# Ten weight conversions moved into the first pair's tiles, the first pair's input sums on VectorE and GpSimd, and routing's vector steps moved to the next pair

## The chip, the cores and the metric

The kernel runs on one core of a Trainium2 chip. The core has TensorE (PE; its weight loads are shown apart as PEld), VectorE (DVE), ScalarE (ACT), GpSimd (POOL) and SyncE (SP, which here issues most DMAs). The metric is device time in microseconds, the median of several runs. All times below are microseconds from the start of the profiled execution, unless it is said otherwise.

## What is computed

Three stages follow each other, in float32:

```python
# 1. linear attention: 4 batches x 8 heads, 576 positions, head size 64, 128 features
proj = q @ w_phi;  proj -= max(abs(proj));  phi = concat(exp(proj), exp(-proj))   # the same for k
kv = phi_k.T @ v;  z = sum(phi_k);  attn = (phi_q @ kv) / (phi_q @ z + 1e-6)
x = attn, 2304 tokens x 512
# 2. dense gated layer, 512 -> 1536 -> 512
g = x @ w_gate;  x2 = (g * sigmoid(g) * (x @ w_val)) @ w_out
# 3. mixture of 8 experts, 512 -> 1024 -> 512: each token goes to its best expert
e = argmax(x2 @ gate);  y = prob[e] * sigmoid(x2 @ output_gate)[e] * (relu(x2 @ w1[e]) @ w2[e])
```

## The kernel before

**Float32 on TensorE by halves.** A float32 operand is split into a rounded high half and a low half, `low = x - high`, and a product is three matmuls: high x high, high x low, low x high. Such a split is called a cut: one ScalarE copy for the high half (`cut`, line 544), one subtraction on VectorE or GpSimd for the low half (`cut_lo`, line 541).

**The attention part** (`first_part`, line 669). Sixteen units, each of two heads of a batch: `qk_mm` (12 small matmuls to a group, three groups, line 330), `qk_sub` (maximum and subtraction on VectorE from PSUM, lines 336 and 339), `k_exp`, `kv_mm`, `tq_mm`, `tq_exp`, `num_mm`, `normalise`, `tx_mm`, and then the attention's output x is stored by pieces. x has six blocks of 384 tokens. Pieces of blocks 0 and 1 stay in SBUF as halves (`x_hi`, line 427, ScalarE; `x_lo`, line 431, VectorE); the others go to DRAM (`x_keep`, `x_store`).

**The weights' conversion** stands between these steps. The weights of the dense layer arrive as 36 chunks of 512 KB (64-bit words, 12 f-tiles of 128 hidden columns times gate, value and output weights). For each: `conv_load` (SyncE, into one of three buffers `ST`), `conv_scale` (ScalarE, to a PSUM bank, line 443), `conv_round` (ScalarE line 452 or GpSimd line 450, into one of four buffers `CP`), `conv_sign` (GpSimd line 458 or VectorE line 460), `conv_bits` (VectorE, line 464) and `conv_add` (GpSimd, line 468). The results lie in `WR[f]`.

The order of all this is written out: `Plan.op` registers each step with its dependencies, and `PLAN_TABLE` lists the steps in the order in which they are issued; a number of 1000 or more takes the step's other engine (`alt`). Each engine runs its steps in that order. Buffers are shared: the input sums S1 and S2 lie where `ST[0]`, `ST[1]` and `CP[0]` were (step `third`, after the last conversions), the weight sums `SS` where the units' inputs were.

**The dense layer** runs over pairs of blocks: (0, 1), (2, 3) and (4, 5), by a scheme with seven products of half size in place of eight (`product`, names A11, A12, S1 to S4, A22; six matmuls of 384 columns each, lines 584 to 586). It needs sums of the weights (`weight_sum`, line 553, four per f-tile) and sums of the input blocks (`SUMS`: S1, S2, S3 and A22). For pair 0 the input sums are matmuls with plus and minus identity matrices into PSUM (`sum_mm`, line 514), then a ScalarE copy (line 760) and a VectorE subtraction (`sum_lo`, line 519). For pairs 1 and 2 they are float32 subtractions on VectorE (`x_sums2`, lines 523 and 533).

`pair(p, rest)` runs the 12 f-tiles of a pair; tile 0 of pair 0 is already in `first_part`, written out product by product, with a cut of its weights for each slot (`pcut`, `sums_of`, `cut_22`). Per tile there are 42 matmuls of 384 columns for the products and nine of 512 columns for the layer's output (`o_tiles`, lines 475 to 477) of block 2p; the hidden values of block 2p+1 are stored to DRAM (`hd`, line 660) and used in `down(p)`, which forms that block's output: 12 steps of nine matmuls, with the input sums of the next pair and the cuts of the hidden values (`cut`, line 541) between them.

**Routing** of a block's tokens is a list of small steps: `post_log` three times, `post_mm`, `post_sum` (transposes and logits), `route_a` (twenty small instructions, most on VectorE), `route_b` (six small matmuls and six VectorE instructions). `down(p)` takes one of them off the list `todo` for each of its steps from the third on (`fill(1)`). Between the products of `pair` the function `rest` calls `fine(2)`, which issues two single instructions of the list `todo`; it is called three times in a tile (group g = 0, 1, 2), in the tiles after the first. `fine(1000)` at the start of `down` issues what is left.

The instructions of `pair` and `down` are not in a written order: the scheduler of the tile framework places them on each engine. The instructions of an engine wait in order.

Of the kernel before, what the change touches and what calls it, by code (L numbers as in the profile page):

```python
# [8 lines left out]
F32 = mybir.dt.float32  # L9
# [44 lines left out]
class Arena:  # L54
# [138 lines left out]
def kernel(ctx, tc, qT, kT, v1, wphi, w1cat, wlog, mw1, mw2, consts, out):  # L193
# [231 lines left out]
    def x_hi(u, piece, b):  # L425
        c, j, o, w = piece
        ACT.activation(XH[:, j, u % 4, o:o + w], PS[:, b, c:c + w], AF.Copy)

    def x_lo(u, piece, b):
        c, j, o, w = piece  # L430
        DVE.tensor_tensor(out=XL[:, j, u % 4, o:o + w], in0=PS[:, b, c:c + w],
                          in1=XH[:, j, u % 4, o:o + w].bitcast(F32), op=ALU.subtract)
# [983 lines left out]
    def down(p):  # L1416
# [8 lines left out]
        for i, f in enumerate(order_):  # L1425
# [18 lines left out]
            if i >= 2:  # L1444
                fill(1)
# [77 lines left out]
```

## Time and profile before

| | us |
|---|---|
| median of 3 runs | 867.95 (867.4 to 870.95) |
| profiled execution | 871.13 |
| its span (first to last instruction) | 869.4 |

Busy time over the span: TensorE 841.3 us (97%), weight loads 735.7 (85%), VectorE 583.6 (67%), ScalarE 501.8 (58%), GpSimd 446.8 (51%). The attention part ends at about 182 us, the first pair's tiles at about 291, its down stage at about 324; pair 1 ends with its down stage at about 474, pair 2 at about 655, and the experts take the rest.

How to read it: these shares are means over stages with different limits, so the busy time has to be asked for by stretch. A busy TensorE is one with a matmul in it, since matmuls overlap. A group of instructions by line gives its count, its busy time, the mean duration of one in nanoseconds, and the idle time of the engine just before, with what ended it. The granted clock of TensorE is 1.00 at its higher level and 0.50 at its lower.

### The profile page before, as it was taken

To read this page: it belongs to the slowest core of one execution; us is meant where nothing else is said; L and a number is where in the kernel's file an instruction comes from. 1 tells how busy PE (TensorE), PEld (TensorE's weight loads), DVE (VectorE), ACT (ScalarE), POOL (GpSimd) and SP (SyncE) were. 2 spreads that over 40 slices of the span, in tenths; PEclk is the share of its full clock that TensorE was granted. 3 is DMA by queue.
4 is the path that set the end of the run, shared out by engine and by line. 5 is a ranking of instruction groups with operands and counts; after the bars stand their busy time and mean duration, and the time that the engine had idled before them with its cause. 6 is when DMAs were issued, how large, how long until landed. Compare 5 with 4: busy or idle time off the path is not lost.

```text
span 869.4 us, 17427 instructions
## 1 busy us (share of the span) xinstructions
PE 841.3 (97%) x6745; PEld 735.7 (85%) x6746; DVE 583.6 (67%) x1105; ACT 501.8 (58%) x936; POOL 446.8 (51%) x421
## 2 busy tenths in 40 slices
PE   8899999989999989999999999999999999999995
PEld 6888998979999869999986999898778888888884
DVE  6898998856556596666659777676686434344693
ACT  4768887846555655555666555555433434344883
POOL 3788888876666655666655666536302212120110
PEclk9999999989999999999999999999999999999998
DMA  8776876710000231000031000006701332010650
GB/s 242 183 236 193 234 241 204 230 50 28 19 19 28 91 109 47 19 19 20 30 95 59 2 1 1 1 0 255 303 1 50 131 99 110 24 51 1 245 208 11
DMA packets 30876, 84.58 MB, mean 97 GB/s; under 512 B 6462, under 2 KB 15678, under 8 KB 29504
## 3 DMA queue, kind: packets, MB, share of 16 engines
q1 hardware_dynamic: 27216, 73.57, 26.5%
q0 software_dynamic: 3200, 9.48, 3.2%
q8 instruction: 55, 0.90, 0.4%
q10 hardware_dynamic: 368, 0.33, 0.2%
q14 instruction: 37, 0.30, 0.1%
HBM read 79.13 MB, written 17.86 MB: 112 GB/s over the span
## 4 chain that ended last, share of the span: by engine, by line
PE 73%; DVE 13%; issue 6%; DMA 3%; ACT 3%; POOL 1%; SPq 0%; POOLq 0%; DVEq 0%; ACTq 0%
PE banks L584 10%; PE banks L586 9%; PE banks L585 9%; PE banks L477 5%; PE banks L476 5%; PE banks L475 5%; PE banks L1204 3%; PE banks L1205 3%; PE banks L1206 3%; PE banks L1220 3%; PE banks L1218 3%; PE banks L1219 3%; DVE arena L336 3%; PE banks L330 2%; PE banks L391 2%
## 5 line engine op out<-in xcount | busy, mean ns | idle before, releaser
L544 ACT ACTIVATE r_dense<-arena 128x512 fp32r<-128x512 f32 (+1 forms) x168 | 100.7, 610 | 135.1 <-PE banks L585 106.4
L553 POOL TENSOR_TENSOR arena<-arena 128x256 f32<-128x256 f32 x144 | 106.6, 751 | 105.5 <-DVE r_dense L541 96.9
L541 POOL TENSOR_TENSOR r_dense<-arena,r_dense 128x512 fp32r<-128x512 f32 x72 | 97.1, 1349 | 60.0 <-ACT r_dense L544 58.4
L541 DVE TENSOR_TENSOR r_dense<-arena,r_dense 128x512 fp32r<-128x512 f32 (+1 forms) x102 | 76.2, 747 | 58.4 <-ACT r_dense L544 58.3
L1194 ACT ACTIVATE arena_r<-arena 128x512 fp32r<-128x512 f32 x64 | 40.3, 633 | 104.5 <-PE banks L1205 49.5
L1197 DVE TENSOR_TENSOR arena_r<-arena,arena_r 128x512 fp32r<-128x512 f32 x64 | 44.2, 693 | 81.4 <-ACT arena_r L1194 79.6
L586 PE MATMUL banks<-arena_r,r_dense 128*128 128x384 f32 x288 | 97.8, 340 | 0.3 <-POOL r_dense L541 0.3
L585 PE MATMUL banks<-arena_r,r_dense 128*128 128x384 f32 x288 | 97.5, 338 | 0.0
L584 PE MATMUL banks<-arena_r,r_dense 128*128 128x384 f32 x288 | 96.8, 343 | 0.6 <-ACT arena L609 0.4
L606 DVE TENSOR_TENSOR banks<-arena,banks 128x384 f32<-128x384 f32 x140 | 77.7, 555 | 9.4 <-ACT arena L609 5.0
L1155 POOL DMA_INDIRECT out_dram<-arena x20 | 21.2, 1059 | 109.6 <-ACT arena L1251 39.6
L613 DVE SCALAR_TENSOR_TENSOR arena<-arena,banks 128x384 f32<-128x384 f32 x70 | 38.8, 554 | 55.3 <-ACT arena L612 54.9
L1150 POOL DMA_INDIRECT ov_gather<-x2d,arena x20 | 21.4, 1071 | 98.3 <-PE banks L1164 57.9
L584 PEld LDWEIGHTS banks<-arena_r,r_dense 128*128 128x128 f32 x288 | 54.4, 189 | 4.8 <-DVE r_dense L606 1.5
L585 PEld LDWEIGHTS banks<-arena_r,r_dense 128*128 128x128 f32 x288 | 54.5, 189 | 3.4 <-issue 0.6
L586 PEld LDWEIGHTS banks<-arena_r,r_dense 128*128 128x128 f32 x288 | 54.6, 190 | 1.8 <-POOL r_dense L541 1.0
L609 ACT ACTIVATE arena<-banks 128x384 f32<-128x384 f32 x105 | 50.5, 482 | 7.2 <-PE banks L586 7.2
L336 DVE TENSOR_REDUCE arena<-banks 128x6 f32<-128x768 f32 x48 | 45.8, 954 | 12.9 <-PE banks L330 11.0
L584 PE MATMUL banks<-ov_pair,r_dense 128*128 128x384 f32 x144 | 51.3, 356 | 0.5
L1204 PE MATMUL banks<-arena_r 128*128 128x512 f32 x128 | 50.2, 393 | 0.8 <-ACT arena_r L1194 0.8
L1206 PE MATMUL banks<-arena_r 128*128 128x512 f32 x128 | 50.0, 391 | 0.0
L1205 PE MATMUL banks<-arena_r 128*128 128x512 f32 x128 | 50.0, 390 | 0.0
(220 smaller groups left out, 2367.7 us busy)
## 6 DMA issues: line engine op xcount, KB each, us to landing
arena<-mw SPq DMA_DIRECT2D x16, 2048.0 KB, 8.4
ov_conv<-w1cat SPq DMA_DIRECT2D x24, 512.0 KB, 5.9
arena<-w1cat SPq DMA_DIRECT2D x12, 512.0 KB, 6.5
arena<-v SPq DMA_DIRECT2D x16, 325.0 KB, 6.6
hd<-arena SPq DMA_DIRECT2D x24, 192.0 KB, 1.8
x2d<-arena SPq DMA_DIRECT2D x18, 256.0 KB, 2.8
arena<-qT SPq DMA_DIRECT2D x15, 288.0 KB, 4.9
arena<-kT SPq DMA_DIRECT2D x15, 288.0 KB, 5.3
```

What stands on the lines that cost most here:

```text
L336: DVE.tensor_reduce(out=MX, in_=ps, axis=AX.X, op=ALU.max, apply_absolute_value=True)
L541: eng.tensor_tensor(out=w[1], in0=src, in1=w[0].bitcast(F32), op=ALU.subtract)
L544: ACT.activation(w[0], src, AF.Copy)
L553: POOL.tensor_tensor(out=o, in0=x, in1=y, op=op)
L584: PE.matmul(ps, w[0][:, c], xh[:, k, :], start=(start and k == 0), stop=False, skip_group_check=True)
L585: PE.matmul(ps, w[0][:, c], xl[:, k, :], start=False, stop=False, skip_group_check=True)
L586: state["pe"] = PE.matmul(ps, w[1][:, c], xh[:, k, :], start=False, stop=(k == 1), skip_group_check=True).ins
L606: DVE.tensor_tensor(out=out_, in0=x, in1=y, op=op)
L609: ACT.activation(out_, x, AF.Copy)
L1204: PE.matmul(ps, wh[:, c], XQH[:, k, :], start=(k == 0), stop=False)
L1205: PE.matmul(ps, wh[:, c], XQL[:, k, :], start=False, stop=False)
L1206: PE.matmul(ps, wl[:, c], XQH[:, k, :], start=False, stop=(k == 3))
```

## The change

Three things.

1. **Ten of the 36 chunks are converted in pair 0's tiles 1 to 10**, one in each (`LATE`, all of f-tiles 8 and 9, two of f-tile 10, two others). Their steps are those of the other chunks, on fixed engines: scaling and rounding on ScalarE after product S3, sign and bits on VectorE after S1, the addition on GpSimd and the next chunk's load at the tile's end. They use bank 7, buffer `ST[2]` and `CP[1..3]`. The first of these loads is issued behind `first_part`.
2. **The input of pair 0 stays in float32** (`X01`, in the place of the weights of f-tiles 8 and 9, with one sum's place `XT1` in f-tile 10's). A piece is one copy (ScalarE, or VectorE). The sums are four float32 subtractions and seven cuts (`less`, `finish`), on VectorE or GpSimd as the table says; the `sum_mm` matmuls and the identity matrices are gone. Weight sums, cuts and the last low halves get the other engine as an alternative.
3. **`down(0)` and `down(1)` issue routing steps only in their steps 2 to 6**: that takes the logits, and leaves `route_a` and `route_b` to the tiles of the next pair. In the last pair `fine` issues three instructions at a call in place of two.

With this goes a new `PLAN_TABLE`. By its entries the steps of `first_part` are, before and after: `conv_scale` 36 and 26 (ScalarE); `conv_round` 16 and 6 (ScalarE), 20 and 20 (GpSimd); `conv_sign` 26 and 21 (GpSimd), 10 and 5 (VectorE); `conv_bits` 36 and 26 (VectorE); `conv_add` 36 and 26 (GpSimd); input halves 12 ScalarE and 12 VectorE before, copies 9 ScalarE and 3 VectorE after; sums of the input 4 of `sum_mm` on TensorE with 4 copies (ScalarE) and 4 low halves (VectorE) before, 4 subtractions (GpSimd), 7 high halves (ScalarE) and 7 low halves (2 VectorE, 5 GpSimd) after; weight sums 8 GpSimd before, 3 GpSimd and 5 VectorE after; low halves of weights 4 VectorE and 5 GpSimd before, 3 and 6 after.

```diff
+    LATE = [24, 25, 27, 28, 26, 30, 31, 29, 33, 35]
+    EARLY = [i for i in range(3 * NFT) if i not in LATE]
+    def stage(i):
+        return ST[2 if i in LATE else EARLY.index(i) % 3]
+    def rounded(i):
+        return CP[1 + LATE.index(i) % 3 if i in LATE else EARLY.index(i) % 4].bitcast(I32)
...
+    def conv_late(f, g):
+        if not 0 < f <= len(LATE):
+            return
+        i = LATE[f - 1]
+        if g == 0:
+            conv_scale(i, 7)
+            conv_round(i, ACT)
+        elif g == 1:
+            conv_sign(i, 7, DVE)
+            conv_bits(i, 7)
+        else:
+            conv_add(i)
+            if f < len(LATE):
+                conv_load(LATE[f])
...
-    SUMS = dict(S1=("+01", "-00"), S2=("+11", "-01", "+00"), A22=("+10", "-11", "+01", "-00"), S3=("+11", "-01"))
-    def sum_mm(name, b): ...
-    def sum_lo(name, b): ...
+    o = offs["WR"] + 8 * 1536
+    X01 = [A[:, o + j * 1536:o + (j + 1) * 1536].rearrange("p (k t) -> p k t", k=4) for j in range(2)]
+    XT1 = A[:, o + 3072:o + 3840].rearrange("p (k t) -> p k t", k=2)
...
+        def finish(name, src, reads):
+            op("ACT", 85, lambda: ACT.activation(opx[name][0], src, AF.Copy), reads, [("fin", name)], due=140)
+            def low(eng):
+                eng.tensor_tensor(out=opx[name][1], in0=src, in1=opx[name][0].bitcast(F32), op=ALU.subtract)
+            op("DVE", 105, lambda: low(DVE), reads + [("fin", name)], [("fin2", name)], due=140, alt=("POOL", 195, lambda: low(POOL)))
+        def less(dst, x, y, reads, writes):
+            def f(eng):
+                eng.tensor_tensor(out=dst, in0=x, in1=y, op=ALU.subtract)
+            op("DVE", 105, lambda: f(DVE), reads, writes, due=130, alt=("POOL", 195, lambda: f(POOL)))
...
     first_part()
+    conv_load(LATE[0])
...
     def rest(p, f, g):
+        if p == 0:
+            conv_late(f, g)
...
-        fine(2)
+        fine(3 if p == NP - 1 else 2)
...
-            if i >= 2:
+            if i >= 2 and (end or i < 7):
                 fill(1)
```

## Rows read from the trace of the kernel before

**Rows 1.** Busy time by stretch (us, PE, PEld, DVE, ACT, POOL; clock; DMA share)

```profile
100.00:120.00 20.00, 20.00 (x482) 18.86 (x480) 19.08 (x33) 17.27 (x35) 18.47 (x12) 1.00 0.88 253
182.00:190.00 8.00, 7.68 (x25) 6.94 (x26) 3.21 (x6) 2.88 (x6) 5.98 (x8) 0.58 0.07 25
220.00:240.00 20.00, 20.00 (x109) 18.98 (x108) 11.42 (x22) 11.69 (x24) 12.37 (x14) 1.00 0.05 20
```

**Rows 2.** The chain that ended last, near 155 (start, us, what)

```profile
154.56 5.18 DMA arena<-w1cat
```

**Rows 3.** TensorE's matmuls near 182 (start, us, what, idle before)

```profile
182.31 0.69 PE L586 MATMUL banks<-arena_r,arena_r 128*128 128x384 f32 x1 [2.33 <-POOL arena_r L541]
182.80 0.52 PE L584 MATMUL banks<-arena_r,ov_pair 128*128 128x384 f32 x1
183.12 0.52 PE L585 MATMUL banks<-arena_r,ov_pair 128*128 128x384 f32 x1
```

**Rows 4.** Busy time by stretch in the two down stages

```profile
303.50:326.00 22.50, 19.62 (x97) 14.30 (x96) 22.29 (x46) 13.04 (x24) 11.60 (x10) 1.00 0.34 105
446.00:476.00 30.00, 28.29 (x140) 21.34 (x139) 25.68 (x50) 18.47 (x35) 16.20 (x13) 1.00 0.21 60
```

**Rows 5.** VectorE's groups by line, 0 to 183.7 (count, busy us, mean ns)

```profile
L464 DVE SCALAR_TENSOR_TENSOR arena<-banks,arena 128x512 int32<-128x512 int32 x36 | 24.3, 681 | 0.1
L431 DVE TENSOR_TENSOR arena_r<-banks,arena_r 128x192 fp32r<-128x192 f32 (+1 forms) x12 | 4.6, 414 | 0.0
L519 DVE TENSOR_TENSOR arena_r<-banks,arena_r 128x768 fp32r<-128x768 f32 x2 | 1.9, 952 | 0.0
```

**Rows 6.** VectorE's groups by line, 296 to 326

```profile
L523 DVE TENSOR_TENSOR arena_r<-arena,arena_r 128x768 fp32r<-128x768 f32 x3 | 4.3, 1434 | 0.0
```

**Rows 7.** GpSimd's groups by line, 0 to 183.7

```profile
L468 POOL TENSOR_TENSOR arena<-arena 128x512 int32<-128x512 int32 x27 | 34.9, 1298 | 11.3 <-DVE arena L464 9.1 <-DVE banks L398 1.9
L458 POOL TENSOR_SCALAR arena<-ov_conv 128x512 int32<-128x512 f32 x17 | 33.7, 1984 | 2.2 <-DMA ov_conv<-w1cat 2.1
L553 POOL TENSOR_TENSOR arena<-arena 128x256 f32<-128x256 f32 x14 | 11.1, 798 | 0.4
```

**Rows 8.** Two VectorE lines, shortest, median and longest ns

```profile
L541 DVE TENSOR_TENSOR r_dense<-arena,r_dense x4: 772/1153/1862, 164.2 to 179.2; 128x512 fp32r<-128x512 f32 x4
L339 DVE TENSOR_TENSOR r_att<-banks,arena x24: 957/957/959, 7.6 to 142.9; 128x768 f32<-128x768 f32 x24
```

**Rows 9.** ScalarE's groups by line, 0 to 183.7

```profile
L443 ACT ACTIVATE banks<-ov_conv 128x512 f32<-128x512 f32 x24 | 15.7, 659 | 2.1 <-DVE arena L339 0.9 <-DVE r_att L339 0.6 <-DMA ov_conv<-w1cat 0.4
L427 ACT ACTIVATE arena_r<-banks 128x192 fp32r<-128x192 f32 (+1 forms) x12 | 4.3, 388 | 1.5 <-PE banks L405 1.4
L760 ACT ACTIVATE arena_r<-banks 128x768 fp32r<-128x768 f32 x2 | 1.6, 801 | 0.7 <-PE banks L514 0.7
```

**Rows 10.** TensorE around sixteen matmuls of the sums

```profile
156.48 3.03 PE L514 MATMUL banks<-arena_r,arena_r 128*128 128x384 f32 x16
159.35 0.49 PE L376 MATMUL banks<-arena 128*128 128x128 f32 x3
```

**Rows 11.** ScalarE, the same cut in two tiles of pair 0

```profile
219.78 0.63 ACT L544 ACTIVATE r_dense<-arena 128x512 fp32r<-128x512 f32 x1 [1.41 <-PE banks L585]
229.17 0.63 ACT L544 ACTIVATE r_dense<-arena 128x512 fp32r<-128x512 f32 x1 [1.40 <-PE banks L585]
```

**Rows 12.** SyncE's stores of hidden blocks in pair 0

```profile
224.77 9.71 SPq L660 DMA_DIRECT2D hd<-arena  x2
```

**Rows 13.** DMA issues of the page (count, KB each, us to landing)

```profile
ov_conv<-w1cat SPq DMA_DIRECT2D x24, 512.0 KB, 5.9
x2d<-arena SPq DMA_DIRECT2D x18, 256.0 KB, 2.8
arena<-mw SPq DMA_DIRECT2D x16, 2048.0 KB, 8.4
```

**Rows 14.** Busy time of routing's recorded steps, first down stage (PE, PEld, DVE, ACT)

```profile
296.00:326.00 30.00, 0.59 (x6) 0.36 (x6) 5.76 (x23) 0.43 (x2) 1.00 0.38 118
```

More of the change, by code (lines that the diff above doesn't have):

```diff
@@ L423, in x_store, with x_copy @@
         SP.dma_start(out=xd[j][:, u % 4, o:o + w], in_=XS[i][:, 0:w])
-    def x_hi(u, piece, b):
+    def x_copy(u, piece, b, eng):
         c, j, o, w = piece
[L427 to L432, printed above, removed]
+        src, d = PS[:, b, c:c + w], X01[j][:, u % 4, o:o + w]
+        if eng is ACT:
+            ACT.activation(d, src, AF.Copy)
+        else:
+            eng.tensor_copy(d, src)
     def warmup(n, b=4):
@@ L456, in conv_sign @@
         if eng is POOL:
-            hi = ST[i % 3].rearrange("p (n two) -> p n two", two=2)[:, :, 1]
+            hi = stage(i).rearrange("p (n two) -> p n two", two=2)[:, :, 1]
             POOL.tensor_scalar(out=wi, in0=hi, scalar1=0.0, scalar2=-2.0 ** 31, op0=ALU.is_lt, op1=ALU.mult)
@@ L504, in third @@
         opx.update(S1=t3[0:2], S2=t3[2:4], w22=(t[:, 2304:2560], AR3[:, 0:256]))
-    SUMS = dict(S1=("+01", "-00"), S2=("+11", "-01", "+00"), A22=("+10", "-11", "+01", "-00"), S3=("+11", "-01"))
-    def sum_mm(name, b):
-        for k in range(2):
-            out_ = PS[:, b + k, :BT]
-            n = 2 * len(SUMS[name])
-            for i, t in enumerate(SUMS[name]):
-                for h in range(2):
-                    PE.matmul(out_, ident_r["+-".index(t[0])], XHL[int(t[1]), int(t[2])][h][:, k, :],
-                              start=(i + h == 0), stop=(2 * i + h == n - 1))
-    def sum_lo(name, b):
-        h, l = opx[name]
-        DVE.tensor_tensor(out=l, in0=PS[:, b:b + 2, :BT], in1=h.bitcast(F32), op=ALU.subtract)
+    o = offs["WR"] + 8 * 1536
+    X01 = [A[:, o + j * 1536:o + (j + 1) * 1536].rearrange("p (k t) -> p k t", k=4) for j in range(2)]
+    XT1 = A[:, o + 3072:o + 3840].rearrange("p (k t) -> p k t", k=2)
     def fin(d, hl):
@@ L552, in weight_sum @@
                        (s4, g1, s2, ALU.subtract))[i]
-        POOL.tensor_tensor(out=o, in0=x, in1=y, op=op)
+        (eng or POOL).tensor_tensor(out=o, in0=x, in1=y, op=op)
     def slot(i):
@@ L738, in first_part @@
                 op(("r2",), 30, second, [], [(x, 1, c) for x in ("kp", "tq", "qp") for c in range(3)] + [("r2d",)], due=145)
-        for i in range(3 * NFT):
-            f, w = divmod(i, 3)
-            due = 15 + 3.5 * i
-            if i >= 3:
-                op(("free", "st", i), 200, lambda: None, [], [("st", i % 3)])
-            op("SP", 150, lambda i=i: conv_load(i), [("queue",)], [("st", i % 3)], due=due - 8)
-            op(("seen", "st", i), 140, lambda: None, [], [("st", i % 3)])
-            h = op("ACT", 65, lambda b, i=i: conv_scale(i, b), [("st", i % 3)], [("cu", i)], 1, due=due)
-            op("ACT", 69, lambda i=i: conv_round(i, ACT), [("st", i % 3)], [("cp", i % 4)], due=due,
+        for n, i in enumerate(EARLY):
+            due = 15 + 3.5 * n
+            if n >= 3:
+                op(("free", "st", n), 200, lambda: None, [], [("st", n % 3)])
+            op("SP", 150, lambda i=i: conv_load(i), [("queue",)], [("st", n % 3)], due=due - 8)
+            op(("seen", "st", n), 140, lambda: None, [], [("st", n % 3)])
+            h = op("ACT", 65, lambda b, i=i: conv_scale(i, b), [("st", n % 3)], [("cu", i)], 1, due=due)
+            op("ACT", 69, lambda i=i: conv_round(i, ACT), [("st", n % 3)], [("cp", n % 4)], due=due,
@@ L753, in first_part @@
         op(("ov",), 30, third, [("r2d",)], [("cp", 0), ("st", 0), ("st", 1), ("ovp",)], due=150)
-        for i, name in enumerate(SUMS):
-            n = len(SUMS[name])
-            h = op("PE", 72 * n, lambda b, name=name: sum_mm(name, b),
-                   [(x, j, v) for x in ("xh", "xl") for j in range(2) for v in range(8)] + [("ident_r",)], [("sum", name)], 2,
-                   due=100 + 8 * i)
-            w = [] if name in ("S3", "A22") else [("ovp",)]
-            op("ACT", 85, lambda b, name=name: ACT.activation(opx[name][0], PS[:, b:b + 2, :BT], AF.Copy),
-               [("sum", name)] + w, [("fin", name)] + [("xh", 1, v) for v in range(8) if name == "S3"], holder=h,
-               due=100 + 8 * i)
-            op("DVE", 95, lambda b, name=name: sum_lo(name, b), [("fin", name)],
-               [("fin2", name)] + [("xl", 1, v) for v in range(8) if name == "S3"], holder=h, due=100 + 8 * i)
+        b11, b21, b12, b22 = (X01[j][:, r:r + 2, :] for j in range(2) for r in (0, 2))
@@ new lines, in less @@
+        def less(dst, x, y, reads, writes):
+            def f(eng):
+                eng.tensor_tensor(out=dst, in0=x, in1=y, op=ALU.subtract)
+            op("DVE", 105, lambda: f(DVE), reads, writes, due=130, alt=("POOL", 195, lambda: f(POOL)))
+        finish("A12", b21, k21)
+        finish("A11", b11, k11)
+        less(XT1, b22, b12, k22 + k12, [("t1",)])
+        finish("S3", XT1, [("t1",)])
+        less(b12, b12, b11, k11 + k12, k12)
+        finish("S4", b22, k22)
+        less(XT1, b22, b12, k22 + k12, [("t1",)])
@@ L765, in first_part @@
+        less(b21, b21, XT1, k21 + [("t1",)], k21)
+        finish("A22", b21, k21)
+        finish("S1", b12, k12 + [("ovp",)])
+        finish("S2", XT1, [("t1",), ("ovp",)])
         d = 150
@@ L781, in cut_22 @@
             op("POOL", 75, lambda: cut_lo(opx["w22"], WR[f][1][:, 256:512], POOL),
-               [("h22",), ("wr", 3 * f + 1)] + [("sum", n) for n in SUMS], [("l22",), ("ident_r",)], due=d)
+               [("h22",), ("wr", 3 * f + 1)], [("l22",)], due=d,
+               alt=("DVE", 45, lambda: cut_lo(opx["w22"], WR[f][1][:, 256:512], DVE)))
         def sp_cut(f, k):
@@ L796, in first_part @@
         tmps = [[("qk", 15, 2), ("kvm", 14)], [("kvm", 14)], [("kvm", 15)], [("kvm", 15)]]
-        xs = [(x, j, v) for x in ("xh", "xl") for j in range(2) for v in range(8)]
         def prod(name, bank_, start, reads, key):
@@ L813, in gt @@
                reads + [("xs", 0)], writes, due=d)
-        b0, b1 = [("xh", 0, v) for v in range(4)], [("xl", 0, v) for v in range(4)]
-        prod("A11", BB, True, b0 + b1, ("B",))
+        prod("A11", BB, True, [("fin", "A11"), ("fin2", "A11")], ("B",))
         ac(sp1, pb, [("B",)] + tmps[0], [("sp1",)])
-        prod("A12", BA, True, b0 + b1, ("A",))
+        prod("A12", BA, True, [("fin", "A12"), ("fin2", "A12")], ("A",))
         dv(pa, sp1, pa, [("sp1",)], [("A",)])
@@ L1344 @@
     POOL.memset(ONE_bf, 1.0)
-    POOL.tensor_copy(ident_r[0], ident)
-    POOL.tensor_scalar(out=ident_r[1], in0=ident, scalar1=-1.0, scalar2=None, op0=ALU.mult)
     POOL.memset(CSB[:, 0, :], 0.0)
```

37 lines of the change are left out of this document (19 added, 18 removed), and 73 rows, old and new, of the table PLAN_TABLE.

## Prediction

> **What bounds the kernel now.** I read the busy time by stretch first, then the chain of work that ended last, then the groups by line of the first 184 us, then single instructions around the places where TensorE stands still.
>
> The kernel has three kinds of stage. In the attention part (to about 182 us) everything is full: between 100 and 120 us TensorE is busy 20.00 us of 20, VectorE 19.08, GpSimd 18.47 and ScalarE 17.27 [rows 1]. No engine alone is the bound there; taking work off one would move the bound to the next. The end of this part is a chain of its own: it goes through the landing of a weight chunk (5.18 us from 154.56) [rows 2], that chunk's conversion and GpSimd's list, on which the low half of the weights of product A22 comes last. TensorE waits 2.33 us for it, and when it starts again its matmuls come every 0.32 us [rows 3]; from 182 to 190 the mean granted clock is 0.58, so for 6.7 of those 8 us it was at the lower of its two levels (1.2 GHz) [rows 1]. In the tiles of a pair (220 to 240 is two of them) TensorE is busy 20.00 of 20 us and the other three 57 to 62% [rows 1]: TensorE bounds, and the others have room. In the "down" stage after pairs 0 and 1 VectorE bounds: of 22.5 us from 303.5 it is busy 22.29, TensorE 19.62 [rows 4].
>
> So the change takes work from the full stage, and from the one that VectorE bounds, and puts it where TensorE alone bounds. What counts is the sum by engine, then what the pair's tiles pay.
>
> **Attention part, by engine.** The instructions of each engine can be counted in the old and the new order table. I price with mean durations; neighbours overlap by some 0.1 us, so these are upper values.
>
> VectorE loses ten bit merges and five sign steps of one size (15 x 0.68 = 10.2 us), twelve low halves of the input (12 x 0.41 = 5.0), four low halves of sums (4 x 0.95 = 3.8) [rows 5] and one cut. It gains three copies (at most 3 x 0.41 = 1.2), two low halves of 768 columns from SBUF, each between 0.95 (the same from PSUM) and 1.43 (three such in the down stage) [rows 5, 6], and five weight sums. Those have run on GpSimd only, 0.80 each [rows 7]; VectorE's nearest row is the 128x512 cut, 0.77 to 1.86 us [rows 8], half of which is 0.39 to 0.93; I take 0.6. The cut that goes is one of that row, at least 0.8. Net 19.8 less 1.2 + 2.5 + 3.0: -13.
>
> ScalarE loses ten scalings and ten roundings (20 x 0.66, of one size: 13.2), twelve high halves (4.7) and four of sums (3.2), and gains nine copies (3.5) and seven high halves of 768 (5.6) [rows 9]: -12.
>
> GpSimd loses ten additions (13.0), five signs (9.9) and five weight sums (4.0); it gains nine subtractions of 768 columns and one cut of 1.3, the price of the addition of that size. No row has 768 columns there. 256 take 0.80 and 512 take 1.30 [rows 7]; the straight line gives 1.8, a plain multiple of the 256 gives 2.4. I take 1.8: 16.2 + 1.3. Net -9.4, and -4 at the dear end.
>
> TensorE loses the 44 matmuls of the sums. Sixteen occupy it from 156.48 to 159.35, 0.18 us each [rows 10]: -7.9. Nothing is added.
>
> All four fall by 8 to 13 us of some 175. With engines full together the stage can't gain much more than the one that falls least: 7.9 by TensorE, 9.4 (4) by GpSimd. The waits between them, for which none is full over the whole part, should shrink in proportion. I take 9. Ten loads leave as well, and the chain's 5.18 us landing is one of the last.
>
> **The hand-over to pair 0.** The low half for A22 now runs on VectorE, and the last chunk's addition stands behind the cuts that tile 0 needs. So the 2.33 us and the lower clock can go: half of 6.7 us is 3.3, less what was waiting anyway, 2.9; together 5.2. But the new tail has a GpSimd list too: from tile 0's first weight sum to the cut that product S3 needs I count fourteen instructions (three sums, three cuts, three additions, two signs, two roundings, one low half), 19 to 20 us by [rows 7]. TensorE's own work beside them is two units less their first products (332 of its instructions, at 482 in 20 us [rows 1]) and four products of six: 18 us. It may be as late. Between 0 and 5.2 I take 3.
>
> **Ten chunks in pair 0's tiles.** A tile takes 9.4 us (one ScalarE cut of a tile to the same cut of the next, 219.78 to 229.17 [rows 11]). Each gets two ScalarE instructions (0.66 each), two on VectorE (0.68 each), one on GpSimd (1.30) and one load. ScalarE is busy 11.7 of 20 us, 5.5 a tile; with 1.3 more that is 73%. It stands 1.40 us before the cut at 229.17 [rows 11] and has two gaps more like it in each tile; TensorE never waits there [rows 1]. Hidden by these gaps: 0. If the two stand ahead of a copy that frees a bank they delay it by 1.3 at most; I take 0.5 us for all ten, with 5 as the far end. VectorE's two read PSUM, and nobody waits for GpSimd's addition within the tile.
>
> The load stands on SyncE behind the store of the tile's hidden block, issued at 224.77 [rows 12]. Its 512 KB took 5.9 us to land in the crowded first part; in quiet stretches 256 KB take 2.8 and 2048 KB 8.4 [rows 13], by the straight line between them 3.6. So it lands about 228.5, while the gap before the cut opens at 227.8: the scaling fits its end, or the next gap. The first load waits at the head of SyncE's queue for the last chunk's rounding on GpSimd; behind it stand the loads of the next blocks' input and the stores of hidden blocks, which nobody reads before the down stage.
>
> **Routing's vector steps.** They are 5.76 us of VectorE in the first down stage [rows 14], and by the code as many instructions in the second. There TensorE stands still for 2.88 us of 22.5 in the first and 1.71 of 30 in the second [rows 4]. That is 4.6 us, all that can come back, as TensorE then bounds; I take 3.7, since some cuts wait for ScalarE too. In pairs 1 and 2 the steps meet a VectorE with the room of [rows 1]; the 32 recorded steps fit the calls (34, of two steps, in the last pair of three) but for some ten, which start the next down stage. Cost 0.2, between 0 and 2.
>
> **The sum.** -9 - 3 + 0.5 - 3.7 + 0.2 = -15.0 us. The profiled execution took 871.1 us (its span is 869.4, with 1.7 around it), which would give 856.1; the median of the three runs is 3.2 us below that execution, so 853.0. Bounds: at best 12 + 5.2 + 4.6, some -21; at the weak ends -4, 0 and -2 with 2 of costs, -4.
>
> **A page that speaks against it.** VectorE's subtraction with one input in PSUM takes 957 to 959 ns in all 24 cases of a row, its cut with both inputs in SBUF from 772 to 1862 ns [rows 8]. The Trainium skill ("GPSIMD Engine Reference", Key points) says that GpSimd shares its SBUF interfaces with VectorE and contends with VectorE instructions that have two SBUF inputs. The trace agrees; by it the change's new VectorE sums and low halves are of the wrong sort, which is rival (a).
>
> **Rivals.**
> (a) *Contention on SBUF inputs makes the first part's end late.* Some ten VectorE instructions there get both inputs from SBUF, beside nine long subtractions on GpSimd. If each costs 1.1 us more (1862 less 772), VectorE's -13 becomes -2 and the first part gains only what the tail does. For it: the range in [rows 8]. Against: the maxima, subtractions and conversions of attention, most of VectorE's list, read PSUM and don't stretch. First part -2 to -5, hand-over 0 to 3: about 861. It decides from 0.5 us apiece.
> (b) *GpSimd's list is the new tail.* At 2.4 us a subtraction, or with the fourteen instructions behind a late chunk, TensorE waits again before S3 and the lower clock comes back. First part -6, hand-over 0: about 859.
> (c) *A chunk's load is late in every tile* (the slower end). ScalarE is in order; if the scaling is placed in the gap at 227.8 and the chunk lands as in the first part, 5.9 us after 225, ScalarE stands till 231, and the copy that frees the bank for S4 comes some 2.6 us late. Ten tiles: +26, so 853 + 26 = 879. It decides from a landing of about 5 us. Against it: 3.6 us by the quiet stretches, and the DMA is 5% busy there [rows 1, 13].
> (d) *The first part doesn't follow*: with four full engines and waits between them the new order is no tighter than the old, and only the down stages gain: about 865.
>
> **Chances.** The forecast (846 to 858) 0.60; (b) 0.12; (a) 0.10; (d) 0.10; (c) 0.08. The range takes in (a), (b) and the best bound: 845 to 864, leaving out (c) and most of (d). A measurement of this kernel tells about 0.5% from no change, 4.3 us: faster means under 863.6. The forecast, (a) and (b) lie there: 0.82; most of (d) and a mild (c) lie within: 0.10; slower 0.08.
>
> **What would show it.** The first product of tile 1 some 12 us earlier; no TensorE wait for a GpSimd cut, and a clock of 1.0, there; tiles of pair 0 still 9.4 us apart, with two more ScalarE instructions; TensorE busy over 21.5 of 22.5 us in the first down stage. Wrong would be: tiles of 10 us or more (ScalarE waiting for a landing), VectorE sums of 0.9 us and more beside GpSimd, or TensorE waiting for GpSimd before S3.

## The result

| | before | after |
|---|---|---|
| median, us | 868.47 (867.40 to 870.95, 4 runs) | 859.75 (858.92 to 860.06, 4 runs) |
| profiled execution, us | 871.13 | 859.70 |
| its span, us | 869.4 | 857.8 |

The ratio is 0.9894, with an interval of [0.9871, 0.9917]. The change makes the kernel 8.7 us faster, where 15 were forecast (853.0): the direction and the range were right, the size was not. The two profiled executions differ by 11.4 us, more than the medians do, since that of before lay 2.7 us above its own median and that of after lies on it.

The busy time of after by stretch, the same columns as [rows 1] and [rows 4] (the down stages now begin 12 us earlier, so their windows do too):

```profile
100.00:120.00 20.00, 18.18 (x415) 16.90 (x413) 17.60 (x31) 15.39 (x28) 16.85 (x11) 1.00 0.72 212
170.00:180.00 10.00, 8.06 (x35) 7.09 (x34) 7.42 (x13) 5.44 (x11) 9.84 (x12) 0.83 0.45 127
180.00:220.00 40.00, 38.29 (x202) 34.71 (x201) 32.65 (x54) 29.01 (x58) 34.19 (x37) 1.00 0.37 116
220.00:240.00 20.00, 19.86 (x107) 18.57 (x106) 14.90 (x24) 12.12 (x25) 15.47 (x17) 1.00 0.09 36
291.50:314.00 22.50, 21.31 (x99) 15.44 (x98) 19.94 (x24) 14.06 (x26) 12.89 (x11) 1.00 0.32 108
434.00:464.00 30.00, 29.71 (x145) 23.16 (x144) 23.75 (x30) 19.86 (x36) 17.57 (x15) 1.00 0.27 86
```

The down stages are as hoped: TensorE 21.31 of 22.5 us where it was 19.62, and 29.71 of 30 where it was 28.29 [rows 4]. New is the stretch from 180 to 220, which by the stores below runs from the end of tile 1 into tile 5: before, TensorE had no idle time in such tiles [rows 1]; here it stands for 1.7 of 40 us, after 1.9 of the 10 us ahead of them. The idle time is not the whole of the loss: 202 matmuls were recorded in these 40 us, where 20 us of before have 109 [rows 1].

Where the time went is best read from one event that comes once in a tile, SyncE's store of the tile's hidden block ([rows 12] is one of before). The first two of before:

```profile
181.27 0.32 SPq L835 DMA_DIRECT2D hd<-arena  x1
196.73 0.32 SPq L660 DMA_DIRECT2D hd<-arena  x1
```

and the first six of after:

```profile
170.69 0.32 SPq L854 DMA_DIRECT2D hd<-arena  x1
183.29 0.33 SPq L668 DMA_DIRECT2D hd<-arena  x1
193.26 0.33 SPq L668 DMA_DIRECT2D hd<-arena  x1
204.51 0.33 SPq L668 DMA_DIRECT2D hd<-arena  x1
214.74 0.33 SPq L668 DMA_DIRECT2D hd<-arena  x1
225.12 8.89 SPq L668 DMA_DIRECT2D hd<-arena  x2
```

Tile 0's store comes 10.6 us earlier, tile 1's 13.4; then the tiles are 9.97, 11.25, 10.23 and 10.38 us apart where before they were 9.4. These four tiles take 4.4 us more than before; in the six after them 1.6 comes back. Followed to the end in the same way (but for rounding, the right column adds up to the difference of the two spans, -11.6):

| stretch | forecast | trace |
|---|---|---|
| to tile 0's store (the first part) | -9 | -10.6 |
| tile 0's store to tile 1's (hand-over) | -3 | -2.9 |
| tiles 2 to 11 of pair 0 (the ten chunks) | +0.5 | +2.8 |
| both down stages | -3.7 | -4.3 |
| tiles of pairs 1 and 2 | +0.2 | -0.6 and +2.7 |
| behind pair 2 | 0 | +1.2 |

**Why the tiles grew.** ScalarE's scalings of the moved chunks, in after (the last column of a row is ScalarE's idle time before it and what ended it):

```profile
172.02 0.63 ACT L448 ACTIVATE banks<-arena 128x512 f32<-128x512 f32 x1 [2.53 <-DMA arena<-w1cat]
177.80 0.64 ACT L448 ACTIVATE banks<-arena 128x512 f32<-128x512 f32 x1 [0.22 <-DVE arena L469]
183.21 0.64 ACT L448 ACTIVATE banks<-arena 128x512 f32<-128x512 f32 x1
188.37 0.63 ACT L448 ACTIVATE banks<-arena 128x512 f32<-128x512 f32 x1 [1.63 <-DMA arena<-w1cat]
194.98 0.64 ACT L448 ACTIVATE banks<-arena 128x512 f32<-128x512 f32 x1 [1.30 <-DMA arena<-w1cat]
```

They are 5.5 us apart in the mean, not 9.4: the code asks for one in each tile, but the scheduler of the tile framework places the steps as early as their data allow, ahead of their tile, and runs two chunks in a tile until all ten are done at about 223 us. ScalarE's instructions wait in order, so it stands for the landing of five of these chunks up to 216 us (and of a sixth, 1.05 us, at 221.61), with the copies that free TensorE's banks behind (its waits from 168 to 216 us: total, times, longest):

```profile
ACT banks L448 <- DMA arena<-w1cat: 6.7, 5, 2.5
```

This is TensorE in tile 1, waiting for such a copy (L617) while ScalarE stood for the first chunk:

```profile
173.97 0.44 PE L592 MATMUL banks<-ov_pair,r_dense 128*128 128x384 f32 x1 [1.94 <-ACT arena L617]
174.25 0.34 PE L593 MATMUL banks<-ov_pair,r_dense 128*128 128x384 f32 x1
174.43 0.41 PE L594 MATMUL banks<-ov_pair,r_dense 128*128 128x384 f32 x1
174.63 0.52 PE L592 MATMUL banks<-ov_pair,r_dense 128*128 128x384 f32 x1
174.95 0.52 PE L593 MATMUL banks<-ov_pair,r_dense 128*128 128x384 f32 x1
```

Right behind the wait its matmuls still come every 0.18 us, from 174.63 on every 0.32, and the granted clock of 170 to 180 is 0.83, so for 3.4 of these 10 us it is at the lower of its two levels (1.2 GHz). The lower clock of [rows 1] and [rows 3] has not gone, it has a new wait ahead of it.

In tiles 2 to 5 the way is longer. TensorE's own waits there are for VectorE (1.0 us from 180 to 220) and for GpSimd (0.7). VectorE's instructions wait in order too, and it stood for a scaling, so that its subtraction for TensorE came late:

```profile
195.65 0.69 DVE L465 TENSOR_SCALAR arena<-banks 128x512 int32<-128x512 int32 x1 [1.95 <-ACT banks L448]
196.86 0.44 PE L592 MATMUL banks<-arena_r,r_dense 128*128 128x384 f32 x1 [0.28 <-DVE r_dense L614]
```

**Theory and rivals for the runs.** Theory: the steps' place, ahead of their tiles, costs some 5 us, in tile 1 and in tiles 2 to 5. Rivals: the added instructions fill the engines wherever they stand, or the loads themselves do it (their traffic beside the tiles). For the 2.7 us of pair 2 the suspect is the three routing steps at a call. A second question is what holds the first part, on which the forecast had "no engine alone".

### The profile page after: what moved, and what is told of

Its sections match the earlier page's. It is cut to its first block, busy times and chain, and to the rows that moved or that the text cites. A ratio compares the mean times of both kernels' runs of the same rounds, so it can differ in the third digit from the quotient of the medians.

```text
span 857.8 us, 17334 instructions
## 1 busy us (share of the span) xinstructions
PE 830.8 (97%) x6701; PEld 724.0 (84%) x6702; DVE 596.0 (69%) x1103; ACT 501.4 (58%) x936; POOL 452.3 (53%) x419
## 5 line engine op out<-in xcount | busy, mean ns | idle before, releaser
L561 POOL TENSOR_TENSOR arena<-arena 128x256 f32<-128x256 f32 x139 | 103.2, 753 | 88.4 <-DVE r_dense L549 83.2
L549 POOL TENSOR_TENSOR r_dense<-arena,r_dense 128x512 fp32r<-128x512 f32 x74 | 99.8, 1350 | 61.8 <-ACT r_dense L552 60.1
L549 DVE TENSOR_TENSOR r_dense<-arena,r_dense 128x512 fp32r<-128x512 f32 (+1 forms) x100 | 82.3, 826 | 40.4 <-ACT r_dense L552 39.2
L617 ACT ACTIVATE arena<-banks 128x384 f32<-128x384 f32 x105 | 50.5, 481 | 8.1 <-PE banks L594 7.8
```

The costliest lines, as they stand in the source:

```text
L549: eng.tensor_tensor(out=w[1], in0=src, in1=w[0].bitcast(F32), op=ALU.subtract)
L561: (eng or POOL).tensor_tensor(out=o, in0=x, in1=y, op=op)
L617: ACT.activation(out_, x, AF.Copy)
```

## Experiments

**1. The conversion steps tied to their tile.** `tie` is the kernel's own: the scheduler may not place the instruction ahead of the TensorE instruction issued last before it.

```diff
         if g == 0:
-            conv_scale(i, 7)
-            conv_round(i, ACT)
+            tie(conv_scale(i, 7))
+            tie(conv_round(i, ACT))
```

> As the changed kernel, but the scaling and the rounding of each of the ten chunks may not be placed on ScalarE ahead of product S3 of their own tile. Theory (the steps run ahead, two chunks to a tile, and ScalarE, which is in order, stands for a chunk that has not landed): ScalarE's waits for a w1cat landing (2.53, 1.63, 1.30 us in tiles 1 to 3) go, TensorE's 1.94 us wait in tile 1 goes and with it the lower clock there, the hidden stores of tiles 1 to 5 stand 9.4 to 9.7 us apart in place of 10.0 to 11.2; the time falls by 3 to 6 us, to about 855. Rival (the added ScalarE, VectorE and GpSimd instructions themselves slow the tiles, by contention for SBUF or by filling the engines): the same loss is only spread over tiles 1 to 10, each at 9.7 to 9.9 us, and the time stays within 1 us of 859.75.

Measured: 854.78 us (852.69 to 857.64, 6 runs), ratio 0.9841 [0.9802, 0.9880]. That is 5.0 us under the median of after. The stores of its first seven tiles:

```profile
171.56 0.32 SPq L854 DMA_DIRECT2D hd<-arena  x1
181.26 0.32 SPq L668 DMA_DIRECT2D hd<-arena  x1
191.90 0.32 SPq L668 DMA_DIRECT2D hd<-arena  x1
201.30 0.32 SPq L668 DMA_DIRECT2D hd<-arena  x1
210.69 0.32 SPq L668 DMA_DIRECT2D hd<-arena  x1
220.08 0.32 SPq L668 DMA_DIRECT2D hd<-arena  x1
229.48 0.32 SPq L668 DMA_DIRECT2D hd<-arena  x1
```

From tile 3 on a tile takes 9.4 us again, with a chunk in it; tile 1 takes 9.7 in place of 12.6. Tile 2, with 10.64, missed the 9.4 to 9.7 that was expected. The scalings are one to a tile and none waits for a landing:

```profile
174.96 0.64 ACT L448 ACTIVATE banks<-arena 128x512 f32<-128x512 f32 x1
184.44 0.64 ACT L448 ACTIVATE banks<-arena 128x512 f32<-128x512 f32 x1
194.79 0.63 ACT L448 ACTIVATE banks<-arena 128x512 f32<-128x512 f32 x1
```

Busy by stretch:

```profile
170.00:180.00 10.00, 9.03 (x47) 7.77 (x46) 7.59 (x13) 5.69 (x12) 9.84 (x12) 1.00 0.41 126
180.00:190.00 10.00, 9.34 (x50) 8.60 (x50) 6.89 (x11) 6.22 (x13) 9.92 (x10) 1.00 0.23 74
220.00:240.00 20.00, 20.00 (x111) 19.20 (x110) 14.06 (x27) 14.22 (x29) 15.33 (x17) 1.00 0.25 79
```

The clock is 1.00 in these stretches. So the place that the scheduler gave two steps is what cost the 5 us. The tie takes away two things at once, the waits for landings and the second chunk in a tile; which of them cost how much the runs don't separate. Nor does the tie decide the clock: other kernels with it are at the lower level in tile 0 (experiment 8). What is left in tiles 0 to 2 is GpSimd, 9.84 and 9.92 of 10 us busy; TensorE waits for its cuts (L549):

```profile
163.22 0.44 PE L594 MATMUL banks<-arena_r,r_dense 128*128 128x384 f32 x1 [1.12 <-POOL r_dense L549]
179.21 0.44 PE L594 MATMUL banks<-arena_r,arena_r 128*128 128x384 f32 x1 [0.94 <-POOL arena_r L549]
187.00 0.50 PE L496 MATMUL banks<-arena_r,r_dense 128*128 128x512 f32 x1 [0.67 <-POOL arena_r L549]
```

**2. The same with one load in place of ten.** The loads of the second to tenth chunk are gone and the first chunk is converted ten times.

```diff
             conv_add(i)
-            if f < len(LATE):
-                conv_load(LATE[f])
```

> As late_tied, but only the first of the ten chunks is loaded: the other nine conversions work on that chunk's data, so that nine loads of 512 KB are left out and the weights of f-tiles 8 to 11 are not the right ones (the routing of tokens then differs, so that only the tiles of pair 0 are read, not the whole time). All engine instructions stay. Theory: with the steps tied, no landing is waited for any more, so the tiles are as long as in late_tied, within 0.1 us. Rival (the loads still cost, by a landing or by DMA traffic): tiles shorter by 0.2 us or more.

Its tokens are routed otherwise, so only pair 0's tiles are compared. Their stores come at 172.61, 181.69, 192.31, 201.70 and 211.10: tile 2 takes 10.62 beside 10.64, and from then on the distances (9.39, 9.40) are those of the run above (9.40, 9.39). There the traffic of the loads costs nothing. Tile 1 is shorter by 0.6 us (9.08 beside 9.70), which would speak for the rival; but tile 0's store comes 1.0 us later and tile 1's 0.4 later, so two traces can't put it down to one load.

**3. Routing's steps back in the down stages** (the third part of the change undone, on after).

```diff
-        fine(3 if p == NP - 1 else 2)
+        fine(2)
...
-            if i >= 2 and (end or i < 7):
+            if i >= 2:
```

> The changed kernel with its third part undone: the down stages take routing steps at every step again, and each call in the last pair issues two. By the two traces the down stages gave 1.4 and 2.9 us and pair 1 another 0.6, while pair 2 lost 2.6: undone, TensorE's idle time in the first down stage is 2.9 of 22.5 us again, pair 2's tiles are 2 to 3 us shorter in all, and the time is 1.5 to 3 us longer, about 862. Rival (the loss in pair 2 comes from elsewhere, the routing part gives its whole 4.3): 864. Rival (it gives nothing on balance): within 0.5 us of 859.75.

Measured: 862.45 us (860.57 to 864.18, 11 runs), ratio 0.9931 [0.9907, 0.9955]; against after (0.9894) this part is worth about 3 us (2.7 by the medians; the intervals overlap a little, but the fastest run here, 860.57, is slower than the slowest of after, 860.06). The first down stage is VectorE's again (compare 291.5 to 314 of after):

```profile
295.00:318.00 23.00, 20.14 (x98) 14.74 (x98) 21.92 (x46) 13.58 (x26) 12.63 (x10) 1.00 0.37 119
```

**4. Two routing steps at a call in the last pair too**, the rest as in after.

```diff
-        fine(3 if p == NP - 1 else 2)
+        fine(2)
```

> The changed kernel with two routing steps at each call in the last pair too, in place of three; the steps that are left, some 44, then run at the start of the last down stage. If three steps at a call are what slows pair 2 (2.6 us over its twelve tiles), the tiles get 2 us back and the last down stage pays 3 to 5 us of VectorE work, of which TensorE feels a part: 859 to 862. If the rate doesn't matter to the tiles: the last down stage alone pays, and the gather of the first rows, which needs the slot map, comes later: 861 to 864.

Measured: 859.82 us (858.13 to 862.59, 6 runs), ratio 0.9894 [0.9857, 0.9932], which is after. The time is the same, but by the trace two changes cancel. From ScalarE's first tanh of pair 2 to its last, in before, after, this run and the run of experiment 3:

```profile
477.60:590.30 112.70, 111.91 (x615) 103.53 (x614) 78.62 (x166) 62.94 (x130) 63.40 (x71) 1.00 0.01 3
462.29:577.81 115.52, 114.26 (x631) 103.83 (x630) 83.53 (x190) 63.61 (x132) 63.80 (x71) 1.00 0.02 4
465.73:574.92 109.19, 108.84 (x600) 102.44 (x599) 75.50 (x166) 62.82 (x130) 63.86 (x71) 1.00 0.01 4
468.53:581.24 112.71, 111.92 (x615) 103.52 (x614) 78.64 (x166) 62.95 (x130) 63.35 (x71) 1.00 0.02 5
```

After's tiles are 2.8 us longer than before's; without the third part they are as long as before; with two steps at a call they are 6.3 us shorter than with three. So the length of these tiles follows the routing steps that are issued in them. What this run saves there it pays behind them: from the last tanh to the end of the span it takes 285.9 us, where after takes 280.0. The first of the two expectations came true, with larger terms on both sides.

This run told one thing more: up to the last pair its instructions are those of after, yet tile 0's store came at 174.23 in place of 170.69. One trace tells the end of the first part to some 3.5 us only; below, the medians decide.

**5 to 7. What holds the first part after the change.** On the kernel of experiment 1, work of one engine is done twice, in place: four 128x768 low halves on GpSimd; eleven bit merges on VectorE; the three score matmuls of the middle chunk of units 3 to 11 on TensorE.

```diff
-                eng.tensor_tensor(out=opx[name][1], in0=src, in1=opx[name][0].bitcast(F32), op=ALU.subtract)
+                for _ in range(2 if name in ("A12", "A11", "S3", "S4") else 1):
+                    eng.tensor_tensor(out=opx[name][1], in0=src, in1=opx[name][0].bitcast(F32), op=ALU.subtract)
```

> The kernel with the tied conversion steps, and the four 128x768 low halves that the new plan gives to GpSimd (A12, A11, S3, S4) computed twice: 7.3 us more of GpSimd (four by 1.82 us) between about 90 and 132 us. Theory (the first part is a web in which GpSimd's list is also the tail: its windows have it 97 to 98% busy from 140 us on): the backlog is not made up, tile 0's store comes 4 to 7 us later than 171.6 and the kernel at 858 to 862. Rival (TensorE and VectorE alone set the first part; GpSimd has slack and its list is late only by chance): store within 1.5 us, kernel 854 to 856.

```diff
-        DVE.scalar_tensor_tensor(out=wi, in0=ui, scalar=3, in1=wi, ...)
+        for _ in range(2 if i in range(2, 24, 2) else 1):
+            DVE.scalar_tensor_tensor(out=wi, in0=ui, scalar=3, in1=wi, ...)
```

> The kernel with the tied conversion steps, and eleven of the conversion's 128x512 bit merges on VectorE done twice (0.68 us each, 7.5 us more of VectorE, spread from about 20 to 150 us; the doubled merge repeats on its own result and changes no bit). Theory (VectorE at 18.5 of 20 us is one of the bounds, with some slack at the unit ends): tile 0's store 3 to 6 us later, kernel 857 to 861. Rival (VectorE is the bound alone): the whole 7.5 us, 862. Rival (VectorE follows TensorE): store within 1.5 us, kernel 854 to 856.

```diff
-        for j in range(3):
+        for j in (0, 1, 2) * (2 if c == 1 and 3 <= u <= 11 else 1):
```

> The kernel with the tied conversion steps, and for nine units (3 to 11) the middle chunk's three score matmuls done twice: 27 more matmuls, 7.8 us more of TensorE at 0.29 us, between about 40 and 125 us. Theory (TensorE at 19.9 of 20 us is one of the bounds in the units' middle): store 5 to 8 us later, kernel 860 to 863. Rival (VectorE or GpSimd is the bound and TensorE is busy only because its matmuls stretch over its waits): store within 2 us, kernel 854 to 857.

(The count in the last was wrong: 54 matmuls were added, 108 recorded instructions of 0.063 us, 6.8 us; the busy time of their line rose by 5.4 us here and by 6.2 in experiment 10.) The table below has what they gave, with the next four.

**8. The five weight sums of VectorE on GpSimd**, on the kernel of experiment 1.

```diff
 PLAN_TABLE (the other engine of five weight sums)
-    ... 1777 ... 1758 ... 1759 ... 1780, 1760 ...
+    ...  777 ...  758 ...  759 ...  780,  760 ...
```

> The kernel with the tied conversion steps, and the five 128x256 weight sums that the new plan gives to VectorE computed by GpSimd, at the same places in the order. VectorE loses five instructions that took 0.4 to 2.0 us each (some 5.5 us in all, between 147 and 160 us); GpSimd gains five by 0.74 us (3.7 us) in a stretch in which it is 98% busy. Theory (GpSimd's list is the tail of the first part and of tile 0): tile 0's store 2 to 4 us later, kernel 856 to 859. Rival (the stretched VectorE instructions are what holds up units 13 and 14): store 1 to 3 us earlier, kernel 851 to 853.5.

Measured: 855.06 us (853.81 to 856.37, 4 runs), ratio 0.9846 [0.9799, 0.9894]: no difference from 0.9841. Tile 0's store is 2.7 us later (174.27), as the theory said, and by tile 2 all of it is back (192.12 beside 191.90). Both expectations missed the total. GpSimd, with five instructions more, is busy 56.8 of the 60 us from 140 (57.1 in experiment 1), and TensorE stands for its cuts as long, only at once: 2.7 us in one wait, where it was 3.1 in four. Behind this wait the clock falls:

```profile
164.51 0.69 PE L594 MATMUL banks<-arena_r,r_dense 128*128 128x384 f32 x1 [2.70 <-POOL r_dense L549]
160.00:170.00 10.00, 6.54 (x21) 5.86 (x22) 3.03 (x4) 4.27 (x11) 9.76 (x10) 0.66 0.41 123
```

The same is seen in experiments 2, 5 and 12: a wait of 1.60, 3.60 and 1.99 us for a GpSimd cut in tile 0, and a clock of 0.83, 0.66 and 0.66 from 160 to 170. Yet tile 2's store comes at 192.31, 191.16 and 191.11. In these kernels the lower clock in tile 0 cost nothing that was left at tile 2.

**9 to 11. The same question on the kernel before.** The same doubling on VectorE and TensorE; on GpSimd four sign steps twice (chunks 9, 12, 16 and 18).

```diff
-            POOL.tensor_scalar(out=wi, in0=hi, scalar1=0.0, scalar2=-2.0 ** 31, ...)
+            for _ in range(2 if i in (9, 12, 16, 18) else 1):
+                POOL.tensor_scalar(out=wi, in0=hi, scalar1=0.0, scalar2=-2.0 ** 31, ...)
```

> The kernel before, with the same eleven bit merges on VectorE done twice (7.5 us more of VectorE in the attention part). Theory (VectorE bounded the attention part before the change as it does after it, where 7.5 us cost 6.4): the kernel some 5 to 7 us slower than before, ratio 1.006 to 1.008. Rival (the prediction's reading, no engine alone is the bound, since TensorE was 20.00 of 20 us busy too): 2 to 4 us, ratio 1.002 to 1.005.

> The kernel before, with the same doubled score matmuls (54 matmuls, by the record 108 instructions of 0.063 us, 6.8 us more of TensorE). Theory (VectorE bounded, TensorE was next): 2 to 3 us slower, ratio 1.002 to 1.004. Rival (TensorE at 20.00 of 20 us was the bound before): 6 to 7 us, ratio 1.007 to 1.008.

> The kernel before, with four of GpSimd's sign steps (chunks 9, 12, 16, 18) done twice: 7.9 us more of GpSimd in the middle of the attention part. Theory (VectorE bounded, GpSimd had room in the units): within 1.5 us of before, ratio 0.999 to 1.002. Rival (GpSimd's list is the tail before the change, so that every microsecond of it counts): 5 to 8 us slower, ratio 1.006 to 1.009.

**12. Less for VectorE**, on the kernel of experiment 1: four sign steps to GpSimd, three input copies to ScalarE.

```diff
-                           alt=("DVE", w, lambda b, x=x: x_copy(u, x, b, DVE)))
+                           alt=("DVE", w, lambda b, x=x: x_copy(u, x, b, ACT)))
...
-               alt=("DVE", 69, lambda b, i=i: conv_sign(i, b, DVE)))
+               alt=("DVE", 69, lambda b, i=i: conv_sign(i, b, POOL if i in (5, 13, 15, 20) else DVE)))
```

> The kernel with the tied conversion steps, and 4.0 us taken off VectorE in the attention part: the four sign steps that the new plan gives it (0.68 us each) go to GpSimd (2.0 each there, 7.9 in all), and its three input copies (1.2 us in all) to ScalarE. Theory (VectorE bounds the first part, 0.85 us for each microsecond, and GpSimd's extra work costs next to nothing): 3 us faster than the tied kernel, 851 to 852.5, ratio 0.980 to 0.982. Rival (TensorE is close behind, so that taking work off VectorE gives back little): within 1 us, 854 to 855.5, ratio 0.983 to 0.986.

The seven together (ratios to the kernel before; the base has 0.9841 [0.9802, 0.9880], tile 4's store at 210.69, or 1 and 224.77):

| run | work added, us | ratio | tile 4's store |
|---|---|---|---|
| tied, GpSimd more | 7.3 | 0.9856 [0.9808, 0.9904] | 210.04 |
| tied, VectorE more | 7.5 | 0.9918 [0.9892, 0.9945] | 215.60 |
| tied, TensorE more | 6.8 | 0.9876 [0.9830, 0.9922] | 213.02 |
| before, VectorE more | 7.5 | 1.0072 [1.0045, 1.0100] | 228.25 |
| before, TensorE more | 6.8 | 1.0049 [1.0030, 1.0067] | 226.87 |
| before, GpSimd more | 7.9 | 1.0017 [0.9997, 1.0036] | 224.51 |
| tied, VectorE less | -4.0 | 0.9868 [0.9844, 0.9892] | 209.90 |

On both kernels the order is the same: 7.5 us on VectorE cost 0.7 to 0.8% (6 to 7 us), 6.8 on TensorE 0.35 to 0.5% (3 to 4 us), and over 7 on GpSimd less than can be told from nothing. So GpSimd has room in the units, full as it looks: in experiment 5 the rival was right. In 6 and 10 the cost came out at the dear end of the theory or just past it, in 7 between theory and rival. VectorE is the tightest. But it does not bound alone: less work on it brought nothing (0.9868, where 0.980 to 0.982 was expected and the rival had 0.983 to 0.986). From 60 to 100 us, first the kernel of experiment 1:

```profile
60.00:100.00 40.00, 39.74 (x881) 36.60 (x877) 37.73 (x64) 30.43 (x61) 34.78 (x22) 1.00 0.72 211
```

and the one with less for VectorE:

```profile
60.00:100.00 40.00, 39.92 (x897) 36.96 (x899) 36.96 (x63) 31.99 (x64) 39.18 (x25) 1.00 0.73 210
```

VectorE is relieved, TensorE was and stays full (by its weight loads too it is within 3% of VectorE: 36.60 beside 37.73), and GpSimd took the steps without effect here. That TensorE is as full is the likely reason, but it isn't shown: the same run gave GpSimd 7.9 us more, TensorE waited 1.99 us for its cut in tile 0, and a small gain may have gone there. The runs don't separate the two.

## Why the prediction was right or wrong

**The number.** 859.75 lies in the range, but not in the forecast's own 846 to 858; it is near the numbers of rivals (b), 859, and (a), 861, and neither mechanism made it, as the rest of this section shows: this nearness is luck. All three signs of being wrong came in some form: tiles of 10 us and more with ScalarE waiting for a landing, VectorE sums of 1.19 us, and a TensorE wait for a GpSimd cut, in tile 0 of after:

```profile
162.35 0.44 PE L594 MATMUL banks<-arena_r,r_dense 128*128 128x384 f32 x1 [1.24 <-POOL r_dense L549]
```

**The first part: right in size, with one bound too many.** Forecast -9; the last unit's `kv_mm` comes 9.0 us earlier and tile 0's store 10.6 (7.0 to 10.6 by the three executions that share after's first part: 170.69, 171.50 and 174.23). "No engine alone is the bound" held: more work costs on VectorE and on TensorE, and less on VectorE gave nothing in the one run that tried it. The step "not much more than the one that falls least" was applied to three engines, and GpSimd wasn't one of them: its -9.4, and the -4 of its dear end, had no place in the sum. TensorE's -7.9 and VectorE's -13 (nearer -10, as its five sums cost more) are left to carry it; neither was taken away alone. Of single prices, the 768-column subtraction on GpSimd is the 1.8 us that was worked out, the weight sum on VectorE twice the 0.6. In after, up to 172 us (count, busy us, mean ns):

```profile
L561 DVE TENSOR_TENSOR arena<-arena 128x256 f32<-128x256 f32 x5 | 5.8, 1186 | 0.0
L549 DVE TENSOR_TENSOR r_dense<-arena,r_dense 128x512 fp32r<-128x512 f32 x2 | 3.5, 1758 | 0.0
L767 DVE TENSOR_TENSOR arena_r<-arena,arena_r 128x768 fp32r<-128x768 f32 x1 | 1.1, 1106 | 0.0
L772 POOL TENSOR_TENSOR arena<-arena 128x768 f32<-128x768 f32 x4 | 7.3, 1821 | 3.0 <-ACT arena L426 2.9
```

**Rival (a) was true as a fact and free as a cost.** The five sums cost 5.8 us of VectorE where 3.0 were booked, so for these five the condition set for (a), "from 0.5 us apiece", was met; the 768-column low halves, 1.0 and 1.1 us, cost no more than was booked. By the Trainium skill ("GPSIMD Engine Reference", Key points) GpSimd contends with just such VectorE instructions, those with two SBUF inputs; the trace agrees, with 0.42 to 2.03 us for one size beside a GpSimd that was 94% busy. But the sums stand in the last units, and giving all five to GpSimd moved the kernel by 0.05%, far less than the interval (experiment 8).

**The hand-over: the number came out, the reason didn't.** -3 was taken between 0 and 5.2, -2.9 measured; that is luck. The clock and the GpSimd cut were to decide; in after a landing decided, and the run of experiment 3, with the same instructions here, has 10.50 us for tile 1 and 13.15 for tile 2. With the steps tied, in experiment 1, the clock stays up and tile 1 takes 9.70 us in place of 15.46, so -5.8, a little past the far end that was worked out (5.2). Of this 1.4 comes back in tile 2, where TensorE waits for GpSimd (the row at 187.00). That is rival (b) in small: TensorE waits for GpSimd's cuts, at a cost of some 1.5 us (9.70 and 10.64 less twice 9.4), not of the whole hand-over. It isn't the length of GpSimd's list that sets these waits: with 7.3 us more of it (experiment 5) tile 2's store comes 0.7 us earlier.

**The ten chunks: the step that failed.** "The load lands about 228.5 while the gap before the cut opens at 227.8" priced the landing well: in after the six scalings that stood for their chunk began 3.5 to 4.5 us after the load's issue (168.47 to 172.02, 184.46 to 188.37, 190.52 to 194.98), and the median of the ten landings is the 3.6 us that was estimated. What failed is that the steps were costed where the source has them. Rows of before could not show where they would go; that the scheduler places the instructions of `pair` was stated in the description, and the step that drew on it ("placed in the gap") was kept for rival (c) alone, at 0.08. Its mechanism is what happened, in tiles 1 to 5 rather than in ten, since two chunks to a tile use them up sooner. It was priced at +26; it cost 2.3 more than the forecast in tiles 2 to 11, and part of the hand-over's gain, 5.0 by the medians. Where the scheduler leaves the steps in their tile, the forecast of +0.5 holds from tile 3 on.

**Routing's steps: right in the down stages, too cheap in pair 2.** -3.7 for both down stages, -4.3 measured, and experiment 3 gives 3 us for the part as a whole. The tiles of pair 1 together are 0.6 us shorter; pair 2 is 2.7 us longer, where both were to cost 0.2 and at most 2. The term counted VectorE's room alone. In pair 2 VectorE has it (83.5 of 115.5 us busy), but TensorE bounds there, and it is busy 2.4 us more than before with the steps in its tiles (114.26 beside 111.91); the waits that the trace names for it come to 0.5 us. With fewer steps in them the tiles are short again (experiments 3 and 4). How much of the 2.4 us is routing's own matmuls and how much products drawn out by the steps was not measured apart. The 1.2 us lost behind pair 2 weren't forecast and weren't looked into.

**The step from the profile to the median.** The sum was taken from the profiled execution and the whole then shifted by the 3.2 us by which that execution lay above its median. The shift didn't carry over: after's profiled execution (859.70) is at its median. Of the 6.8 us between 853.0 and 859.75, the shift is 3.2 and the sum 3.6, and these are the chunks (2.3), pairs 1 and 2 (1.9) and the stretch behind them (1.2), less what the first part and the downs gave more (2.2); the last 0.4 is the hand-over's 0.1, what lies outside the spans, and rounding.

**What the change could have given.** With two calls of `tie` it is at 854.78, within 2 us of the forecast and faster than both kernels.

## What to carry to other kernels

Work moved into a stage that a scheduler orders goes where its data allow, not where the source has it: before costing such a step at nothing, ask what lets it start, and if that is a transfer, tie the step to work of its own place. A full engine is priced best by giving it more work, and less, since the busy shares of the units (60 to 100 us) did not tell the prices: GpSimd, 87% busy, cost nothing that could be told from noise, VectorE, 94%, nearly its full price, TensorE, 99%, about half. And a step that goes to a stage where TensorE bounds has to be priced by what it does to TensorE, not by the room of its own engine. And a forecast is a difference: the distance between a profiled execution and its median belongs into the range, not into the sum.

## What was not expected of the hardware

- VectorE's subtraction of 128x256 with both inputs in SBUF took 0.42 to 2.03 us in five cases beside a GpSimd that was 94% busy from 150 to 170 us; the longest is five times the shortest.
- The first 3.4 us at the lower clock in after followed a TensorE wait of 1.94 us in tile 1. In the kernel of experiment 1 waits of 1.12 and 0.94 us in tiles 0 and 1 left it at 1.00; in that of experiment 6 a wait of 1.03 us that ended at 168.21, behind two of 0.75 and 0.30, was followed by matmuls every 0.32 us, and the clock is 0.91 from 160 to 170 and 0.92 from 170 to 180. So the length of one wait does not tell whether the clock falls.
- A lower clock of 0.66 from 160 to 170 in experiments 5, 8 and 12 left tile 2's store where it was in experiment 1, within 0.8 us.
- Two executions with the same instructions up to the last pair ended the first part 3.5 us apart (170.69 and 174.23).
